# A gated GELU MLP on one core: eight transposing loads issued by ScalarE, 1 MB reloads ahead of the planes' stores, and four smaller moves in the order

## The chip, the cores and the metric

The kernel runs on one core of one Trainium2 chip. The metric is the device time of one execution in microseconds (us). Six actors matter: TensorE (PE, with its weight loads shown apart as PEld), VectorE (DVE), ScalarE (ACT), GpSimd (POOL), SyncE (SP, which issues nearly all DMAs in this kernel), and the 16 DMA engines that carry the transfers.

## The reference

For x of 2048 x 1024, W_gate and W_up of 1024 x 3584 and W_down of 3584 x 1024, all bf16:

```
g = x @ w_gate
u = x @ w_up
h = gelu_tanh(g) * u
out = h @ w_down
```

## The kernel before

The 2048 rows are handled in two passes of 1024 rows, and each pass in two halves c = 0, 1 of 512 rows. A pass has two stages: the units, which compute h for 256 columns of W_gate and W_up at a time (14 units), and `down`, which multiplies h by W_down. Within a stage the kernel doesn't do the plain eight block products of a 2 x 2 split of the matrices. It uses a scheme of seven products (Strassen's, in Winograd's form), and in some units and in one part of `down` a second level of it inside. So PE does fewer products, and the others form sums: VectorE and GpSimd make the operands (`s1`, `s2`, `s3`, `s4` of the weights, `t1` to `t4` of x; `s`, `q`, `m` in `down`), and ScalarE makes copies of PSUM banks (`snap`: u, p, u2, p5, z) and casts (`sa`, `tb`). Names of tiles in the profile are these names. Every matmul is of 128 x 128 by 128 x 512 and is recorded at line 145; VectorE's sums are recorded at line 121, GpSimd's at 124, ScalarE's copies at 133 or 138, its gelu at 213.

Most operands live in a ring of 36 slots of 2 KB a partition (`slot`, pool k) and one of 13 (pool s). A slot is given to the next tile when the last reader of the tile before it is done; where that reader is a store to DRAM, the next writer waits for the store.

*Order.* The work is emitted under a manual schedule: what an engine does stands in its queue in the order in which the program emits it, and an engine waits at each instruction for the semaphores that it needs. For `down` an agenda maps a step number to actions: `at(last, step, what, ...)` puts an action at a step of pass one (last = 0) or pass two (last = 1), and `step()` runs them in turn between the groups of products. The lists at the top give the steps: `LAST12` (`load12`, reloads of m, the sums of W_down that pass one left in DRAM as td), `LAST12S` (`make12`), `RAW73` (`fetch73`: the second halves of W_down), `LAST73` (`make73`: per j three VectorE sums s3, t3, s4 and one ScalarE cast tb). A transfer's completion is counted by one of eight semaphores, given out in turn over all DMAs that SP and ScalarE issue; a DMA waits for the one that had its semaphore before.

*The units that the change touches.* Pass two begins with unit 0's and unit 1's "raw" products (`raw_of`: plain first products of a unit whose sums aren't there yet; a closure finishes them with a sum, a gelu and a multiply). `prepare` runs inside a unit behind the p5 copies, `aside(part)` at marked points of it. `fetch_p5` reloads tiles that pass one stored in DRAM as pd. `need12(n)` fetches the n-th piece of W_down's first half (tile raw, line 689 in the page).

*The end of `down` in pass two.* It has the seven-product scheme over 14 values of j, and one of its seven products is itself done by the second level (`apart`). In order on PE: the raw first products; three groups of the q12 products; `apart` with its inner products K1, K2, K22, K3, K4 (with `step()` between); the remaining q12 products; then the q73 products for j = 0 to 13, and the last products bank by bank, each followed by a store of the output.

The four parts of the second-level product have to be transposed before they can be added to the output. `out(k, ...)` forms part k by two VectorE sums, `planes` splits the 32-bit numbers into two planes of 16 bits (a ScalarE copy) and stores them to DRAM (`pt[k]`, line 734); `turn_back(quad, n)` loads them back with a DMA that transposes (line 744; eight per quad, quad 0 holding parts 0 and 1, quad 1 parts 2 and 3); `join` puts the planes together again on ScalarE (tile gt). Parts 1 and 3 go to two fixed tiles (`pls`, `gs`), part 2, whose call gives no place, to tiles of the ring; part 0 is from pass one. `fetch_u3` reloads u3, the value to which gt is added (`put_0`, VectorE, tile st, and a store); `join_1` joins quad 1.

```
        out(1, Y, u, 0)
        inner(X, TI[K3], S1i, False, step=step)
        z = [snap(X[d], "z") for d in D]
        out(3, X, v, 2)
        inner(Y, TI[K4], S2i, True, step=step)
        out(2, Y, z)
```

`BIG12L = (5, 9)`: j = 5, 6 and j = 9, 10 are reloaded by one 1 MB load each (tile w of a pool of three, line 631 in the page), j = 7 and 8 by 512 KB loads (tile m, line 636), the others by 256 KB loads (tile q, line 642). The stores of the planes (`pt<-xT`, `pt<-pl`) and all these loads are in SP's one queue.

Of the kernel before, what the change touches and what calls it, by code (L numbers as in the profile page):

```python
# [10 lines left out]
def kernel(  # L11
# [23 lines left out]
    nc = tc.nc  # L35
# [36 lines left out]
    D2 = 2 * P  # L72
    ORD4 = [*range(0, NJ, 2), *range(1, NJ, 2)]
    MSTEPS = 17
    LAST12 = [14, 15, 16, 29, 30, 43, 43, 43, 44, 47, 47, 49, 50, 51]
    LAST12S = [16, 18, 20, 34, 37, 40, 43, 45, 47, 49, 51, 53, 55, 57]
    BIG12L = (5, 9)
    RAW73 = [41, 41, 41, 41, 48, 48, 50, 53, 55, 57, 60, 62, 64, 64]
    LAST73 = [52, 53, 55, 57, 59, 61, 63, 65, 66, 68, 70, 71, 72, 73]
    LATE3 = 6  # L80

# [28 lines left out]
    def slot(shape, dtype, name, sums=False):  # L110
        return (spool if sums else kpool).tile(shape, dtype, name=name, tag="s" if sums else "k")
# [8 lines left out]
    def dve(out, a, b, op):  # L120
        nc.vector.tensor_tensor(out=out, in0=a, in1=b, op=op)  # L121
# [14 lines left out]
    def snap(ps, name, at=None):  # L136
        t = slot([P, N], f32, name) if at is None else at
        nc.scalar.copy(out=t, in_=ps)  # L138
        return t
# [590 lines left out]
    def planes(k, d, at, pl=None):  # L730
        if pl is None:
            pl = slot([P, 2, N], u16, "pl")
        nc.scalar.copy(out=pl, in_=at.bitcast(u16).rearrange("p (n l) -> p l n", l=2))
        nc.sync.dma_start(
            out=pt[k].rearrange("(l d p) n -> d p l n", l=2, d=2)[d], in_=pl
        )
# [3 lines left out]
    def turn_back(quad, n):  # L740
        if n == 0:
            turned["tp", quad] = wpool.tile([P, NS, 2, N], u16, name="w")
        half, i = n // NS, n % NS
        nc.sync.dma_start_transpose(  # L744
            out=turned["tp", quad][:, i, half], in_=pt[2 * quad + half][:, i * P : (i + 1) * P]
        )

# [57 lines left out]
    def at(last, step, what, *args):  # L805
        agenda.setdefault((last, int(step)), []).append((what, args))

    for last in (False, True):
        if last:
            at(1, -1, load_ti, K1)  # L810
            at(1, -1, load_ti, K2)
            at(1, -1, load_a0)
        for n in range(NJ):
            at(last, max(-1, 2 * n - 8 if n < 10 else n + 1), need12, n)
        for j in range(NJ):
            at(last, (LAST12 if last else AT12)[j], load12, j, last)
            at(last, (LAST12S if last else AT12S)[j], make12, j, last)
            at(last, RAW73[j] if last else AT73[j] - 3, fetch73, j)
            at(last, (LAST73 if last else AT73)[j], make73, j, last)
# [7 lines left out]
    for i in range(NI):  # L827
        at(1, 2 * i, make_si, i)
    for n in range(2 * NS):
        at(1, 52 + n, turn_back, 0, n)  # L830
        at(1, 60 + n, turn_back, 1, n)
    for i in range(NS):
        at(1, 64 + 2 * i, fetch_u3, i)
        at(1, 68 + 2 * i, put_0, i)
        at(1, 70 + i, join_1, i)
    moves = [(c, ko) for ko in range(KH) for c in range(2)]
    moves += [(c, ko) for c in (1, 0) for ko in range(KH, NKB)]
    sa = {}
# [11 lines left out]
    def inner(ps, lhs, rhs, start, stop=True, step=None):  # L850
        for i in range(NI):
            if step and i % 2 == 0:
                step()
            for d in range(2):
                matmul(
                    ps[d], lhs[i][:, d * P : (d + 1) * P], rhs[i],
                    start and i == 0, stop and i == NI - 1,
                )

    def apart(c, step):  # L860
        X, Y = c[:2], c[2:]
        D = range(2)
        into(X, m1s)
        inner(Y, TI[K1], S1i, True, step=step)
        v = [snap(Y[d], "v") for d in D]
        inner(X, TI[K2], S2i, False, step=step)
        for i in range(NI):
            dve(S1i[i], A0[2 * i], h(1, 2 * i, 1), SUB)
        u = [snap(X[d], "u") for d in D]
        inner(Y, TI[K22], S4i, False, step=step)  # L870
        for i in range(NI):
            nc.scalar.copy(out=S2i[i], in_=h(1, 2 * i + 1, 1))

        pls = xpool.tile([P, 4, 2, N], u16, name="xT0")
        gs = xpool.tile([P, 4, N], f32, name="xT1")

        def out(k, ps, other, at=None):
            g = [slot([P, N], f32, "g") if at is None else gs[:, at + d] for d in D]
            for d in D:
                dve(g[d], ps[d], other[d], ADD)  # L880
            for d in D:
                planes(k, d, g[d], None if at is None else pls[:, at + d])

        out(1, Y, u, 0)
        inner(X, TI[K3], S1i, False, step=step)
        z = [snap(X[d], "z") for d in D]
        out(3, X, v, 2)
        inner(Y, TI[K4], S2i, True, step=step)
        out(2, Y, z)

    def down(ip, e, c, last, more):
        I = range(NS)
# [199 lines left out]
    def raw_of(u, e):  # L1092
        p1 = raw_products(e, K, xT, W(u))
        return lambda: finish_raw(u, K, p1)
# [33 lines left out]
    for ip in range(NPASS):  # L1128
        with tc.manual_schedule(engines={ENG.Activation}):
            if ip == 0:  # L1130
                ws = {1: w, 2: ahead}
                late = lambda: add(cc, nxt["p1"])
            else:
                fetch_ti(0), fetch_ti(1)
                raw_of(0, F)()
                rest(0)
                t["t3"] += t["how"]["t3"](t, range(2, KH))
                t.make("t4")
                raw_of(1, C)()
            for u in range(1 if ip == 0 else 0, NU):  # L1140
                if upgraded(u):
                    if u % 2:
# [52 lines left out]
                first = (ip, u) == (0, 1)  # L1195

                def prepare():
                    if first or (ip, u) == (1, 0):
                        pool_behind(t["t4"][-1])
                    if ip == 0 and u in (2, 3):  # L1200
                        lo_part(u - 2, 3, K)
                    if u + 1 < NU:
                        nxt["s"] = make_s(W(u + 1), pool, nxt.get("s"))
                    if (ip, u) == (0, FIRST - 2):
                        fetch_wd(JS[FIRST][:1])
# [10 lines left out]
                def aside(part):  # L1216
                    if first and part < 0:
                        rest_of_0(part + 2)
                    if ip == 1:
                        for i in {(0, 0): (2,), (1, 0): (3,), (1, 1): (4,), (2, 0): (5, 6)}.get((u, part), ()):  # L1220
                            fetch_ti(i)
                    if ip == 1 and part == 1:
                        if u == 0:
                            rest(1)
                        if u == 3:
                            send_a0()
                    if part == 0 and u + 2 < NU:
                        W(u + 2)
                        if ip and upgraded(u + 2):
                            fetch_p5(u + 2)  # L1230
                        if (ip, u) == (0, 1):
                            load_lo()
                    if first and part == 0:
                        t.make("t4")
# [84 lines left out]
```

## Time and profile before

| | |
|---|---|
| time, median of 3 runs | 545.5 us (544.61 to 547.37) |
| the profiled execution's own time | 548.82 us |
| its span in the profile | 547.0 us |
| mean granted clock of TensorE | 0.994 |
| PE busy | 531.8 us, 97% of the span, 2354 instructions |
| DVE, ACT, POOL busy | 404.8, 301.7, 268.4 us (74, 55, 49%) |
| DMA | 126.09 MB, mean 230 GB/s |
| largest kinds of load | W_down pieces x72 of 256 KB; W_gate and W_up x27 each of 512 KB |

The span is that of the profiled execution, and its rows are times from the span's start. Pass two's `down` takes the last part of it, and the end stage of which the prediction speaks, from the reloads of `apart` on, is about the last 75 us. PE's busy time counts a matmul's records until their modelled end, so a slow clock shows as busy time and not as idle. A row of the timeline gives start, length, engine, line, operation, out<-in, the count, and in brackets the idle time before it with what ended it. SPq is SP's queue, where a DMA's row is the issue; a row with DMA in place of the engine is the transfer itself.

### The profile page before, as it was taken

How to read it: one execution, taken by the hardware profiler on the slowest of the kernel's cores; microseconds unless marked ns; L12 is line 12 of the kernel's file. 1: busy time of each engine (PE TensorE's matmuls, PEld its weight loads, DVE VectorE, ACT ScalarE, POOL GpSimd, SP SyncE). 2: the span in 40 equal slices, each digit the busy share in tenths (PEclk: the TensorE clock that was granted, in tenths of full speed). 3: DMA queues.
4: the chain of work that ended last, by engine and by line, in shares of the span. 5: the costliest groups of instructions: out<-in, count | busy, mean ns of one | idle time of the engine just before them, and what ended most of it. 6: DMA issues, size and time to landing. Idle time of an engine off the chain costs nothing.

```text
span 547.0 us, 7735 instructions
## 1 busy us (share of the span) xinstructions
PE 531.8 (97%) x2354; PEld 375.4 (69%) x2375; DVE 404.8 (74%) x645; ACT 301.7 (55%) x544; POOL 268.4 (49%) x259
## 2 busy tenths in 40 slices
PE   8999999999999999999999999999999999997977
PEld 4568686868686864688867685776766854875855
DVE  2988768787777796659698786658657697895766
ACT  2567686968686821016666675565665611561560
POOL 1079968979698940000007978877897300000000
PEclk9999999999999999999999999999999999999988
DMA  9795227676666899999996899828443996589663
GB/s 242 160 245 162 77 80 267 204 278 208 215 237 235 285 386 382 326 303 216 246 303 212 277 333 347 232 58 232 118 114 115 315 353 227 192 286 318 166 145 125
DMA packets 141161, 126.09 MB, mean 230 GB/s; under 512 B 31680, under 2 KB 119232, under 8 KB 141120
## 3 DMA queue, kind: packets, MB, share of 16 engines
q1 hardware_dynamic: 141120, 125.60, 75.9%
q8 instruction: 19, 0.31, 0.2%
q14 instruction: 22, 0.18, 0.1%
HBM read 86.38 MB, written 31.06 MB: 215 GB/s over the span
## 4 chain that ended last, share of the span: by engine, by line
PE 86%; DMA 8%; DVE 2%; SPq 2%; issue 1%; ACT 0%; DVEq 0%; ACTq 0%
PE bank L145 86%; DMA raw<-in_w_down_dram 2%; DMA w<-td 2%; DVE q L121 1%; DMA hL<-w 1%; DMA pt<-pl 1%; DMA w<-in_w_up_dram 1%; DMA u<-ud 1%; SPq L618 0%; SPq L744 0%; DVE st L121 0%; SPq L992 0%; SPq L689 0%; ACT xT L138 0%; SPq L756 0%
## 5 line engine op out<-in xcount | busy, mean ns | idle before, releaser
L124 POOL TENSOR_TENSOR s<-w 128x512 fp32r<-128x512 bf16 x102 | 117.5, 1170 | 49.8 <-DMA w<-in_w_gate_dram 36.1
L145 PE MATMUL bank<-t,s 128*128 128x512 f32 x528 | 126.5, 392 | 1.1 <-ACT u L138 1.1
L145 PEld LDWEIGHTS bank<-t,s 128*128 128x128 f32 x528 | 99.0, 188 | 22.8 <-ACT u L138 1.5
L145 PE MATMUL bank<-xT,w 128*128 128x512 bf16 (+1 forms) x489 | 108.2, 376 | 1.4 <-DVE hT L121 0.3
L145 PEld LDWEIGHTS <-w 128*128 128x128 bf16 x504 | 47.8, 98 | 59.0 <-issue 5.4
L213 ACT ACTIVATE g<-sum 128x512 f32<-128x512 f32 x81 | 51.5, 636 | 65.3 <-DVE sum L121 63.0
L138 ACT COPY p<-bank 128x512 f32<-128x512 f32 x98 | 55.0, 590 | 46.6 <-PE bank L145 46.6
L145 PE MATMUL bank<-q 128*128 128x512 f32 x224 | 59.5, 404 | 5.3 <-DVE q L121 5.2
L121 DVE TENSOR_TENSOR hT<-g,bank 128x512 bf16<-128x512 f32 x72 | 49.0, 687 | 16.8 <-ACT g L213 11.1
L124 POOL TENSOR_TENSOR s<-w,s 128x512 fp32r<-128x512 bf16 x50 | 57.8, 1173 | 0.4
L124 POOL TENSOR_TENSOR s<-s,w 128x512 fp32r<-128x512 f32 x50 | 57.5, 1168 | 0.4
L121 DVE TENSOR_TENSOR bank<-bank,p 128x512 f32<-128x512 f32 x74 | 51.3, 695 | 6.5 <-PE bank L145 6.0
L145 PE MATMUL bank<-t,sa 128*128 128x512 f32 x216 | 54.9, 397 | 0.0
L145 PEld LDWEIGHTS bank<-q 128*128 128x128 f32 x224 | 42.6, 192 | 17.5 <-DVE q L121 8.1
L145 PE MATMUL bank<-tb,s 128*128 128x512 f32 x216 | 54.2, 393 | 0.0
L199 POOL COPY seen<-t 128x1 f32<-128x1 f32 x2 | 0.4, 183 | 108.4 <-DVE t L121 108.4
L145 PEld LDWEIGHTS bank<-t,sa 128*128 128x128 f32 x216 | 40.6, 188 | 9.1
L121 DVE TENSOR_TENSOR sum<-bank,p 128x512 f32<-128x512 f32 x54 | 37.0, 686 | 13.1 <-PE bank L145 11.4
L145 PEld LDWEIGHTS bank<-tb,s 128*128 128x128 f32 x216 | 40.6, 188 | 8.8
L138 ACT COPY u<-bank 128x512 f32<-128x512 f32 x62 | 35.3, 595 | 15.1 <-PE bank L145 11.7
L121 DVE TENSOR_TENSOR sum<-bank,u 128x512 f32<-128x512 f32 x27 | 18.5, 685 | 19.0 <-PE bank L145 16.3
L145 PE MATMUL bank<-raw,hT 128*128 128x512 bf16 x140 | 31.4, 379 | 1.1 <-DMA raw<-in_w_down_dram 0.9
(121 smaller groups left out, 727.6 us busy)
## 6 DMA issues: line engine op xcount, KB each, us to landing
raw<-in_w_down_dram SPq DMA_DIRECT2D x72, 256.0 KB, 5.9
w<-in_w_gate_dram SPq DMA_DIRECT2D x27, 512.0 KB, 4.5
w<-in_w_up_dram SPq DMA_DIRECT2D x27, 512.0 KB, 6.0
td<-m SPq DMA_DIRECT2D x11, 768.0 KB, 5.2
q<-td SPq DMA_DIRECT2D x28, 256.0 KB, 5.6
pd<-xT SPq DMA_DIRECT2D x10, 512.0 KB, 5.8
w<-td SPq DMA_DIRECT2D x5, 1024.0 KB, 9.4
p<-pd SPq DMA_DIRECT2D x20, 256.0 KB, 4.9
```

Of the source, the lines that this page charges most:

```text
L121: nc.vector.tensor_tensor(out=out, in0=a, in1=b, op=op)
L124: nc.gpsimd.tensor_tensor(out=out, in0=a, in1=b, op=op)
L138: nc.scalar.copy(out=t, in_=ps)
L145: nc.tensor.matmul(ps, lhsT=lhs, rhs=rhs, start=start, stop=stop, skip_group_check=True)
L199: nc.gpsimd.tensor_copy(out=seen, in_=tile[:, :1].bitcast(f32))
L213: nc.scalar.activation(g, src, ACT.Gelu_apprx_tanh)
```

## The change

Six edits to the order of emission, none to what PE does or to its order:

1. *Pass one's and pass two's first-half loads* (`need12`): the load n = 8 comes two steps earlier.
2. *Pass two, unit 0*: the finishing of unit 1's second raw product (its sums, its gelu, its multiplies) moves from the place right behind the products into unit 0's `prepare`, behind unit 0's p5 copies.
3. *Pass two, units 2 and 3*: `fetch_p5` for units 4 and 5 moves from `aside(0)` to `aside(1)`.
4. *Reloads in `apart`*: the two 1 MB loads are emitted right behind the inner products K22 and K3, and the 512 KB loads of j = 7 and 8 at step 41, ahead of the first store of the planes; before, they stood at steps 43 and 47.
5. *Part 2* goes to the places of part 1 in the two fixed tiles `gs` and `pls` in place of four tiles of the ring.
6. *The way back*: quad 0's eight transposing loads are issued by ScalarE, two a step in steps 52 to 55; quad 1's by SP a step earlier than before; `fetch73` comes up to four steps earlier; the four u3 loads come one a step in 66 to 69, and `put_0` and `join_1` alternate in steps 70 to 77.

```diff
--- before.py
+++ after.py
@@ -72,10 +72,10 @@
     D2 = 2 * P
     ORD4 = [*range(0, NJ, 2), *range(1, NJ, 2)]
     MSTEPS = 17
-    LAST12 = [14, 15, 16, 29, 30, 43, 43, 43, 44, 47, 47, 49, 50, 51]
+    LAST12 = [14, 15, 16, 29, 30, None, None, 41, 41, None, None, 49, 50, 51]
     LAST12S = [16, 18, 20, 34, 37, 40, 43, 45, 47, 49, 51, 53, 55, 57]
     BIG12L = (5, 9)
-    RAW73 = [41, 41, 41, 41, 48, 48, 50, 53, 55, 57, 60, 62, 64, 64]
+    RAW73 = [40, 40, 40, 40, 48, 48, 49, 50, 52, 53, 55, 57, 60, 60]
     LAST73 = [52, 53, 55, 57, 59, 61, 63, 65, 66, 68, 70, 71, 72, 73]
     LATE3 = 6
 
@@ -741,7 +741,8 @@
         if n == 0:
             turned["tp", quad] = wpool.tile([P, NS, 2, N], u16, name="w")
         half, i = n // NS, n % NS
-        nc.sync.dma_start_transpose(
+        queue = nc.sync if quad else nc.scalar
+        queue.dma_start_transpose(
             out=turned["tp", quad][:, i, half], in_=pt[2 * quad + half][:, i * P : (i + 1) * P]
         )
 
@@ -811,9 +812,10 @@
             at(1, -1, load_ti, K2)
             at(1, -1, load_a0)
         for n in range(NJ):
-            at(last, max(-1, 2 * n - 8 if n < 10 else n + 1), need12, n)
+            at(last, max(-1, (2 * n - 8 if n < 10 else n + 1) - 2 * (n == 8)), need12, n)
         for j in range(NJ):
-            at(last, (LAST12 if last else AT12)[j], load12, j, last)
+            if (LAST12 if last else AT12)[j] is not None:
+                at(last, (LAST12 if last else AT12)[j], load12, j, last)
             at(last, (LAST12S if last else AT12S)[j], make12, j, last)
             at(last, RAW73[j] if last else AT73[j] - 3, fetch73, j)
             at(last, (LAST73 if last else AT73)[j], make73, j, last)
@@ -827,12 +829,12 @@
     for i in range(NI):
         at(1, 2 * i, make_si, i)
     for n in range(2 * NS):
-        at(1, 52 + n, turn_back, 0, n)
-        at(1, 60 + n, turn_back, 1, n)
+        at(1, 52 + n // 2, turn_back, 0, n)
+        at(1, 59 + n, turn_back, 1, n)
     for i in range(NS):
-        at(1, 64 + 2 * i, fetch_u3, i)
-        at(1, 68 + 2 * i, put_0, i)
-        at(1, 70 + i, join_1, i)
+        at(1, 66 + i, fetch_u3, i)
+        at(1, (70, 72, 74, 76)[i], put_0, i)
+        at(1, (71, 73, 75, 77)[i], join_1, i)
     moves = [(c, ko) for ko in range(KH) for c in range(2)]
     moves += [(c, ko) for c in (1, 0) for ko in range(KH, NKB)]
     sa = {}
@@ -868,25 +870,26 @@
             dve(S1i[i], A0[2 * i], h(1, 2 * i, 1), SUB)
         u = [snap(X[d], "u") for d in D]
         inner(Y, TI[K22], S4i, False, step=step)
+        load12(BIG12L[0], True)
         for i in range(NI):
             nc.scalar.copy(out=S2i[i], in_=h(1, 2 * i + 1, 1))
 
         pls = xpool.tile([P, 4, 2, N], u16, name="xT0")
         gs = xpool.tile([P, 4, N], f32, name="xT1")
 
-        def out(k, ps, other, at=None):
-            g = [slot([P, N], f32, "g") if at is None else gs[:, at + d] for d in D]
+        def out(k, ps, other, at):
             for d in D:
-                dve(g[d], ps[d], other[d], ADD)
+                dve(gs[:, at + d], ps[d], other[d], ADD)
             for d in D:
-                planes(k, d, g[d], None if at is None else pls[:, at + d])
+                planes(k, d, gs[:, at + d], pls[:, at + d])
 
         out(1, Y, u, 0)
         inner(X, TI[K3], S1i, False, step=step)
+        load12(BIG12L[1], True)
         z = [snap(X[d], "z") for d in D]
         out(3, X, v, 2)
         inner(Y, TI[K4], S2i, True, step=step)
-        out(2, Y, z)
+        out(2, Y, z, 0)
 
     def down(ip, e, c, last, more):
         I = range(NS)
@@ -1136,7 +1139,7 @@
                 rest(0)
                 t["t3"] += t["how"]["t3"](t, range(2, KH))
                 t.make("t4")
-                raw_of(1, C)()
+                nxt["c11"] = raw_of(1, C)
             for u in range(1 if ip == 0 else 0, NU):
                 if upgraded(u):
                     if u % 2:
@@ -1195,6 +1198,8 @@
                 first = (ip, u) == (0, 1)
 
                 def prepare():
+                    if (ip, u) == (1, 0):
+                        nxt.pop("c11")()
                     if first or (ip, u) == (1, 0):
                         pool_behind(t["t4"][-1])
                     if ip == 0 and u in (2, 3):
@@ -1220,14 +1225,14 @@
                         for i in {(0, 0): (2,), (1, 0): (3,), (1, 1): (4,), (2, 0): (5, 6)}.get((u, part), ()):
                             fetch_ti(i)
                     if ip == 1 and part == 1:
+                        if u < 4 and upgraded(u + 2):
+                            fetch_p5(u + 2)
                         if u == 0:
                             rest(1)
                         if u == 3:
                             send_a0()
                     if part == 0 and u + 2 < NU:
                         W(u + 2)
-                        if ip and upgraded(u + 2):
-                            fetch_p5(u + 2)
                         if (ip, u) == (0, 1):
                             load_lo()
                     if first and part == 0:
```

## The prediction

> **What bounds the kernel now.** I read the page's busy shares and the summary of the chain that ended last, then the waits, then the timeline wherever TensorE (PE) waited.
>
> ```profile
> PE 531.8 (97%) x2354; PEld 375.4 (69%) x2375; DVE 404.8 (74%) x645; ACT 301.7 (55%) x544; POOL 268.4 (49%) x259
> ...
> PE 86%; DMA 8%; DVE 2%; SPq 2%; issue 1%; ACT 0%; DVEq 0%; ACTq 0%
> ```
>
> ```profile
> PE bank L145 <- DVE q L121: 5.2, 6, 1.9
> PE bank L145 <- DMA w<-td: 1.1, 1, 1.1
> PE bank L145 <- ACT u L138: 1.1, 1, 1.1
> PE bank L145 <- DMA raw<-in_w_down_dram: 0.9, 1, 0.9
> PE bank L145 <- DVE hT L121: 0.3, 1, 0.3
> ```
>
> PE is busy for 97% of the span, and its queue of products is the same in both programs (the change reorders only ScalarE, VectorE and SyncE). So what can be won is PE's waits for the others (us in total, times, longest): 0.9 + 1.1 + 0.3 = 2.3 us ahead of the end stage, and 1.1 + 5.2 = 6.3 in it. One loss has no wait; the table by stretches (busy time, then granted clock, DMA share, GB/s) shows it:
>
> ```profile
> 510.00:520.00 10.00, 10.00 (x46) 8.15 (x45) 5.94 (x10) 4.78 (x8) 0.00 (x0) 1.00 0.74 176
> 530.00:537.00 7.00, 6.06 (x14) 4.14 (x14) 7.00 (x13) 1.73 (x2) 0.00 (x0) 0.52 0.29 95
> ```
>
> The waits of that last stretch alone:
>
> ```profile
> PE bank L145 <- DVE q L121: 0.9, 2, 0.6
> ```
>
> From 530 to 537 the granted clock is 0.52. 14 products ran; at the rate of 510 to 520 (46 in 10 us) they take 3.0 us. Of the other 4.0, 0.9 are waits, which leaves some 3.0 to the slow clock. The ceiling of the change is 2.3 + 6.3 + 3.0 = 11.6 us.
>
> **Part by part. One load earlier in pass one.** PE's 0.9 is its wait for the fifth second-half load of W_down, which SyncE (SP) issued behind three stores. The change puts that load (n = 8) ahead of them.
>
> ```profile
> 204.75 1.42 SPq L618 DMA_DIRECT2D td<-m  x3
> 206.22 4.08 SPq L689 DMA_DIRECT2D raw<-in_w_down_dram  x4
> ```
>
> It is issued 1.47 us earlier (206.22 - 204.75), the stores 0.5 us later; VectorE, which waits for the stores' slots, feeds products several steps on. The next load keeps its place and is then the latest. 0 to 0.9, taken: 0.9.
>
> **Second raw product.** PE's 1.1 is a wait for ScalarE's copy u, and that stands behind a gelu:
>
> ```profile
> 291.50 0.63 ACT L213 ACTIVATE g<-sum 128x512 f32<-128x512 f32 x1 [4.69 <-DVE sum L121]
> 292.04 1.05 ACT L138 COPY u<-bank 128x512 f32<-128x512 f32 x2
> ```
>
> In the changed order both u copies and both p copies come before that gelu. The u copies need only products that ended before PE stopped. VectorE's multiply waits for the gelu about 0.6 us longer, and PE's next use of VectorE's sum is two groups of eight products (16 at 10 / 46 us, 3.5 us) on. GpSimd's first sum still waits for VectorE's t4, as before. Gain 1.1. **Loads of p5**: moved behind the stores of tid in units 2 and 3. PE's 0.3 (for VectorE's hT) came from a slot that such a store held, and the stores now go first; the p5 tiles are first read in unit 4. -0.3 to 0.3, taken: 0.3. Sum so far 2.3.
>
> **Reloads ahead of the planes' stores.**
>
> ```profile
> 469.49 1.92 SPq L662 DMA_DIRECT2D raw<-in_w_down_dram  x4
> 479.58 1.33 SPq L734 DMA_DIRECT2D pt<-xT  x2
> 481.00 0.43 SPq L631 DMA_DIRECT2D w<-td  x1
> ```
>
> ```profile
> 476.00:480.00 4.00, 4.00 (x20) 3.30 (x19) 2.88 (x5) 4.00 (x8) 0.00 (x0) 1.00 0.03 11
> 480.00:500.00 20.00, 18.76 (x81) 14.84 (x80) 14.06 (x23) 8.79 (x13) 0.00 (x0) 1.00 1.00 342
> ```
>
> ```profile
> 462.44 21.81 PE bank L145 x96
> 484.25 10.85 DMA w<-td
> ```
>
> Before, SP stood from 471.4 (469.49 + 1.92) at the first plane store, which waits for ScalarE until 479.58; both 1 MB loads and two 512 KB loads were queued behind it. The DMA engines idled from 476 to 480 (share 0.03), then ran full for 20 us (1.00, 342 GB/s), and the second 1 MB load, issued at 484.25, landed at 495.1: PE's wait of 1.1. In the changed order the 512 KB loads wait only for VectorE's sums, the first 1 MB load for the last product of K22, the second for that of K3. VectorE's rows date these:
>
> ```profile
> 473.30 0.68 DVE L121 TENSOR_TENSOR s<-a,hL 128x512 fp32r<-128x512 bf16 x1
> 473.90 0.68 DVE L121 TENSOR_TENSOR q<-hT,hL 128x512 fp32r<-128x512 bf16 x1
> 474.62 0.69 DVE L121 TENSOR_TENSOR q<-q,hT 128x512 fp32r<-128x512 f32 x1
> 477.09 1.29 DVE L121 TENSOR_TENSOR xT<-bank,u 128x512 f32<-128x512 f32 x2 [1.78 <-ACT s L872]
> ...
> 481.02 1.29 DVE L121 TENSOR_TENSOR xT<-bank,v 128x512 f32<-128x512 f32 x2
> ```
>
> The last sum s is done by 474; out(1) begins behind K22 at 477.1 and out(3) behind K3 at 481.0. So the second 1 MB load goes at 481 at the latest, 3 us earlier, and about 4 us x 342 GB/s = 1.4 MB of the queue ahead of it has landed by 480. It lands near 490, against a use that moves to 493.9 (495.1 less 1.1): the 1.1 goes. Price if not: 1.1.
>
> **Planes of the third part in pls and gs.** These tiles came from the ring of slots; VectorE's next operand then had to wait until the store left its slot:
>
> ```profile
> 500.55 0.69 DVE L121 TENSOR_TENSOR q<-hT,hL 128x512 fp32r<-128x512 bf16 x1 [6.32 <-DMA pt<-pl]
> ```
>
> With the parts in two fixed tiles that wait is gone; VectorE runs 6.3 us ahead, and two of PE's six waits for its q go:
>
> ```profile
> 502.03 1.21 PE L145 MATMUL bank<-q 128*128 128x512 f32 x4 [1.13 <-DVE q L121]
> ...
> 505.16 1.21 PE L145 MATMUL bank<-q 128*128 128x512 f32 x4 [1.00 <-DVE q L121]
> ```
>
> 1.13 + 1.00 = 2.1.
>
> **Eight transposes on ScalarE, u3 at the end.** PE's other four waits for q (5.2 - 2.1 = 3.1 us), and with them the slow clock (3.0), come from VectorE standing for its first u3:
>
> ```profile
> 524.03 0.69 DVE L121 TENSOR_TENSOR st<-gt,u 128x512 bf16<-128x512 f32 x1 [8.09 <-DMA u<-ud]
> ```
>
> ```profile
> L744 SPq DMA_TRANSPOSE w<-pt x16: 1127/1158/1258, 497.9 to 524.1; - x16
> ...
> DMA to landing us min/median/max: 2.7/3.1/5.2
> ```
>
> SP needs 1.158 us for each transposing load, 18.5 us for sixteen. Eight go to ScalarE, which has 9.3 us less idle then. But the order of the changed program gives SP's first transpose a wait for the landing of ScalarE's last ones, and behind it in SP's queue stand the last four W_down loads, seven more transposes, the four u3 loads and the stores of the output. So u3 is the thing that is late next:
>
> ```profile
> 487.56 2.18 ACT L677 CAST xT<-raw 128x512 fp32r<-128x512 bf16 x4
> ```
>
> ```profile
> 516.39 1.95 SPq L662 DMA_DIRECT2D raw<-in_w_down_dram  x4
> ```
>
> ```profile
> u<-ud SPq DMA_DIRECT2D x4, 256.0 KB, 3.7
> ```
>
> ```profile
> 543.62 0.69 DVE L121 TENSOR_TENSOR st<-bank,u 128x512 bf16<-128x512 f32 x1 [1.14 <-PE bank L145]
> ```
>
> From ScalarE's first transpose: eight issues 9.3, three casts among them 1.6 (2.18 / 4 each), landing 3.1, SP's four loads 1.95, its eight transposes 9.3, u3's landing 3.7: 29 us. It can begin at 489.7, when ScalarE is free (487.56 + 2.18), and at the latest at 497.9, where the first transpose was before; each waits for one of eight completion lanes, that is for loads issued just before, which land 4 us earlier than they did. I take 491, near the early end: u3 at 520. After it VectorE has ten operations at 0.6 us (473.90 - 473.30) before PE can start the last of the q73 products (j = 13): 526. PE ended at 543.6, where VectorE's last store begins. With 11.6 us gone it would end at 532.0 and want that one 36 products earlier, at 0.227 us (21.81 / 96) 8.2 us: 523.8. So 2.3 us of new wait; 1.0 from 489.7, 9.2 from 497.9. The price of an issue on ScalarE no row shows. Nearest is SP's 1.158; below it nothing is won past the 2.3; twice that costs 9.3 more.
>
> Sum: 2.3 + 1.1 + 2.1 + 3.1 + 3.0 = 11.6, less 2.3 is 9.3 us. The profiled execution took 548.82 (span 547.0 and 1.8 around it), so 539.5. The median of the runs, 545.5, is 3.3 below it; some of the waits may be the profiled execution's own, so I take 9.0 off the median: **536.5 us**.
>
> **Weighed against the Trainium skill.** The trace's clock fell after waits of at most 1.9 us at a time. The Trainium skill (TensorE: Matmul & The Clock Gate, Part 1) says that an idle window of about 3.4 us closes the gate; here the measurement differs, since no single wait is that long. By that rule a new wait of 2 to 6 us spread over several products costs no clock, and the first rival below would come out at 539.7. The added wait of SP's first transpose is what the skill (DMA: Bandwidth & Descriptors, on two transposing streams in flight) demands; no run here yet shows two streams.
>
> **Rivals.** *u3 too late* (0.18): lanes land late and ScalarE starts at 494.5. u3 at 523.5, VectorE at 529.5, 5.8 us of wait, and the clock falls again: 11.6 - 5.8 - 3.0 = 2.8 us, 542.7. For it: the chain of 29 us is all in order. Against: the idle DMA engines at 476 to 480. Its spread is 539 to 545, half of it past 0.5%.
>
> *ScalarE pays* (0.12, slower): an issue holds ScalarE 2.3 us. T from 491: 18.4 + 1.6 + 3.1 + 1.95 + 9.3 + 3.7 puts u3 at 529, VectorE at 535: 11.4 of wait and 3.0 of clock, 14.4 against 11.6, so 548.3. It turns at 2.0 us an issue. For it: nothing is shown of ScalarE's issues. Against: SP's sixteen lie within 1.127 and 1.258.
>
> *The end does not move* (0.10): the queue of loads is as full as before, or the end stage's waits are mostly the profiled execution's; only the 2.3 us ahead of it stay: 543.2, within 0.5%.
>
> **How the numbers follow.** Forecast 0.60, with its own range 533.5 (no new wait, 11.6 and a little off) to 539.5. The whole range goes to 543.5, over the third rival and most of the first; left out are the second and the upper tail of the first, under 0.2. A measurement of this kernel tells about 0.5% (2.7 us) from nothing. Faster 0.60 + 0.09 = 0.69, same 0.09 + 0.10 = 0.19, slower 0.12.
>
> **What would show it.** Right: no wait of PE for raw in pass one or for ScalarE's u; SP's m and w loads issued from 472 to 481; no wait of VectorE for pt; DMA_TRANSPOSE on ScalarE's queue at about 1.2 us each from 490 to 502; clock 1.00 to the end; PE's last product near 534. Wrong: a wait of VectorE for u3 over 5 us, transposes on ScalarE near 2 us or their first one past 496, PE waiting for ScalarE's copies of u2 or p5 behind them, or a clock of 0.5 again.

## The result, and the profile after

| | before | changed |
|---|---|---|
| median of 14 runs of each | 546.58 us (544.61 to 548.1) | 542.01 us (539.99 to 544.74) |
| ratio | | 0.9921, 95% interval 0.9903 to 0.9939 |
| profiled execution, its own time | 548.82 | 539.99 |
| its span, its mean clock | 547.0, 0.994 | 538.2, 1.000 |
| second profiled execution: time, span, clock | 547.38, 545.6, 0.994 | 542.64, 540.9, 0.994 |

The change gains 4.6 us (0.8%). That is the way that was forecast and inside the stated range, but only about half of the 9.0 us. The two profiled executions of the first pair are 8.8 us apart, nearly the forecast's 9.3, but that is luck: before's was slower than each of its 14 other runs, the changed kernel's the fastest of its 14. The second pair is 4.7 apart, like the medians.

The page of the changed kernel, busy shares and the summary of the chain:

```profile
PE 529.5 (98%) x2375; PEld 374.2 (70%) x2375; DVE 404.0 (75%) x645; ACT 302.2 (56%) x544; POOL 268.3 (50%) x259
...
PE 91%; DVE 3%; SPq 3%; DMA 1%; issue 1%; ACT 1%; DVEq 0%; ACTq 0%
```

TensorE's waits in the changed kernel from 480 us on are one line. In this execution the three waits ahead of the end stage, the one for the 1 MB reload and the two behind VectorE's wait for pt are gone:

```profile
PE bank L145 <- DVE q L121: 3.9, 3, 2.1
```

The table by stretches; the first two rows answer to those of before:

```profile
476.00:480.00 4.00, 4.00 (x19) 3.31 (x18) 3.93 (x7) 3.73 (x6) 0.00 (x0) 1.00 0.96 364
480.00:500.00 20.00, 19.81 (x86) 15.69 (x85) 18.89 (x32) 6.01 (x9) 0.00 (x0) 1.00 1.09 298
510.00:520.00 10.00, 9.94 (x43) 7.73 (x42) 0.00 (x0) 2.25 (x4) 0.00 (x0) 1.00 0.59 122
527.00:534.00 7.00, 7.00 (x32) 5.73 (x31) 7.00 (x13) 0.81 (x1) 0.00 (x0) 1.00 0.55 186
```

The DMA engines, idle from 476 to 480 before (0.03), now run (0.96). From 510 to 520 VectorE does nothing (0.00): it stands at its first u3, which this row of the timeline shows,

```profile
520.06 0.69 DVE L121 TENSOR_TENSOR st<-gt,u 128x512 bf16<-128x512 f32 x1 [10.56 <-DMA u<-ud]
```

and SyncE's rows show why:

```profile
503.49 1.16 SPq L745 DMA_TRANSPOSE w<-pt  x1
504.75 1.94 SPq L662 DMA_DIRECT2D raw<-in_w_down_dram  x4
506.74 9.75 SPq L745 DMA_TRANSPOSE w<-pt  x7
516.59 1.95 SPq L757 DMA_DIRECT2D u<-ud  x4
```

SyncE's eight transposes and four loads go first, and u3 leaves at 516.59. VectorE's last store, which marks TensorE's end, begins 14.7 us after the u3 addition:

```profile
534.78 0.69 DVE L121 TENSOR_TENSOR st<-bank,u 128x512 bf16<-128x512 f32 x1 [0.23 <-PE bank L145]
```

So u3 is late next, as the forecast and its first rival said, and the time, 542.0, is near that rival's (542.7), though not by its dates: u3 came at 520, not at 523.5. (The third rival's 543.2 is near it too, but by that one nothing in the end stage would have changed.) The experiments ask what the gain came from, and what the wait for u3 costs.

### The profile page after: what moved, and what is told of

Its sections match the earlier page's. It is cut to its first block, busy times and chain, and to the rows that moved or that the text cites. A ratio compares the mean times of both kernels' runs of the same rounds, so it can differ in the third digit from the quotient of the medians.

```text
span 538.2 us, 7762 instructions
## 1 busy us (share of the span) xinstructions
PE 529.5 (98%) x2375; PEld 374.2 (70%) x2375; DVE 404.0 (75%) x645; ACT 302.2 (56%) x544; POOL 268.3 (50%) x259
## 4 chain that ended last, share of the span: by engine, by line
PE 91%; DVE 3%; SPq 3%; DMA 1%; issue 1%; ACT 1%; DVEq 0%; ACTq 0%
PE bank L145 91%; DVE q L121 2%; SPq L745 2%; DMA w<-in_w_up_dram 1%; DVE xT L121 1%; DMA u<-ud 1%; ACT s L875 0%; SPq L995 0%; SPq L757 0%; DVE st L121 0%; ACT u L138 0%; SPq L662 0%; SPq L1014 0%; DVEq L121 0%; ACTq L138 0%
## 5 line engine op out<-in xcount | busy, mean ns | idle before, releaser
L145 PE MATMUL bank<-xT,w 128*128 128x512 bf16 (+1 forms) x504 | 110.4, 376 | 0.1
L145 PE MATMUL bank<-q 128*128 128x512 f32 x224 | 57.4, 394 | 4.1 <-DVE q L121 3.9
L133 ACT CAST tb<-raw 128x512 fp32r<-128x512 bf16 x20 | 12.4, 627 | 36.5 <-DMA raw<-in_w_down_dram 30.1
L133 ACT CAST sa<-w 128x512 fp32r<-128x512 bf16 x54 | 30.7, 616 | 2.7 <-DMA out_dram<-st 2.7
```

The costliest lines, as they stand in the source:

```text
L133: nc.scalar.copy(out=t, in_=src)
L145: nc.tensor.matmul(ps, lhsT=lhs, rhs=rhs, start=start, stop=stop, skip_group_check=True)
```

## The experiments

Each ratio is to runs of before that stood beside the experiment on the same chip; their medians lay between 545.35 and 546.81. Two kernels measured on different chips are best compared by their ratios. An interval in brackets behind a ratio is its 95% interval.

### Second executions of both

No edit.

> The kernel before once more, unchanged, for a second profiled execution beside the one that the forecast was summed from. Theory A (the waits of the first profile are there in every execution): TensorE waits again about 0.9 for raw, 1.1 for u, 0.3 for hT, 1.1 for the 1 MB reload and 5.2 for q, 8.6 us in all. Theory B (some of them are that execution's own): the 0.9 and the 0.3 are smaller or gone, as they are in the run with the three edits ahead of the end stage undone, the other 7.4 within 1.5 us. The clock lies between 0.994 and 1.00.

> The changed kernel once more, unchanged, for a second profiled execution. Theory A: VectorE stands 9 to 12 us for its first u3 and TensorE waits 3.5 to 5 us for q, again between 517 and 527; where its mean clock is under 1.00, the stretch of low clock lies right behind those waits. Theory B (the first profile's waits aren't typical): under 2 us of waits for q.

The two took 547.38 and 542.64 us. TensorE's waits in the second execution of before:

```profile
PE bank L145 <- DVE q L121: 5.6, 5, 2.5
PE bank L145 <- ACT u L138: 1.1, 1, 1.1
PE bank L1054 <- PEq L1303: 0.8, 1, 0.8
PE bank L145 <- DMA w<-td: 0.6, 1, 0.6
PE bank L145 <- DMA raw<-in_w_down_dram: 0.4, 1, 0.4
```

and of the changed kernel:

```profile
PE bank L145 <- DVE q L121: 2.5, 3, 1.6
PE bank L145 <- DMA q<-td: 0.9, 2, 0.5
PE bank L1057 <- PEq L1308: 0.8, 1, 0.8
PE bank L145 <- DMA raw<-in_w_down_dram: 0.4, 1, 0.4
```

A wait of 0.4 for raw is there although the first edit is in place, so that this edit isn't shown to remove such waits. For line 145 that is 7.7 (5.6 + 1.1 + 0.6 + 0.4) against 3.8 (2.5 + 0.9 + 0.4): 3.9 of the 4.7 us. In the first pair it was 8.6 against 3.9, 4.7 us; the rest of its 8.8 is mostly clock, (1.000 - 0.994) x 547 = 3.3. The second execution of the changed kernel has the slow stretch again; it begins among the three waits behind the late u3, which end at 522.72, 524.53 and 526.93:

```profile
510.00:520.00 10.00, 10.00 (x45) 8.11 (x44) 0.79 (x2) 3.38 (x4) 0.00 (x0) 1.00 0.58 105
524.00:531.00 7.00, 6.14 (x14) 4.36 (x15) 7.00 (x13) 4.51 (x5) 0.00 (x0) 0.52 0.25 86
```

14 products in 7 us at 0.52, as in the first profile of before. Over its 14 runs the changed kernel's clock is 0.9957 in the mean, an estimated loss of 2.3 us (0.0043 x 541); that of before beside the experiments is 0.995 to 0.997, 1.7 to 3 us. So on average the change doesn't win the clock back. The estimate is rough: of the 72 runs of before beside the experiments, the 35 with a clock of 0.993 or 0.994 took 547.2 us in the mean and the 15 with 1.000 took 545.0, which is 2.1 us and not 3.3.

### The wait for u3 taken away

Edits on the changed kernel, `put_late`, `u3_first` and both together:

```diff
 # put_late
-        at(1, (70, 72, 74, 76)[i], put_0, i)
-        at(1, (71, 73, 75, 77)[i], join_1, i)
+        at(1, 73 + i, put_0, i)
+        at(1, 74 + i, join_1, i)
 # u3_first
-        at(1, 66 + i, fetch_u3, i)
+        at(1, 57 + i // 2, fetch_u3, i)
```

> The changed kernel with VectorE's four u3 additions moved behind the operands of j = 11, 12 and 13 (ScalarE's joins follow them); nothing else differs. Theory A (u3 is late next): in the changed kernel's trace VectorE stands 10.6 us for the first u3 and TensorE waits 3.9 us for the operands behind it, and the slow clock of most of its executions follows from that wait. Then no wait of TensorE for q is left, the clock is 1.00, and the median falls by 4 to 6 us, to 536 to 538. Theory B (what is missing to the forecast is only that the profiled execution of before was a slow one): the waits have other causes too, the median stays within 1.5 us of 542.0.

> The changed kernel with the four loads of u3 issued by SyncE ahead of its eight transposes, not behind them; nothing else differs but the slots that this moves. Theory A: u3 lands before VectorE wants it (509), the wait of 10.6 us falls to what the joins of the first quad leave, under 2 us; 3 to 6 us faster than the changed kernel, 536 to 539. Theory B: within 1.5 us of 542.0. Theory C (the ring of slots): four slots taken some 10 us earlier hold up VectorE's operands of j = 5 to 8, 541 to 545.

> The changed kernel with both: u3 loaded ahead of the second quad, and VectorE's u3 additions behind the operands of j = 11 to 13. Theory A (TensorE has no wait left with either): the two don't add up, 535 to 536.5, and TensorE's end is the end. Rival (the stores of the output and the joins are next): the later additions push VectorE's last stores past TensorE's end, 536.5 to 538.

They took 536.84 us (ratio 0.9829, 0.9803 to 0.9856), 535.78 (0.981, 0.9784 to 0.9835) and 535.26 (0.9804, 0.9775 to 0.9832). Theory A held each time; the second is 0.2 us below its range. With u3 first, all that is left of TensorE's waits in the whole profiled execution is

```profile
PE bank L1057 <- PEq L1308: 0.8, 1, 0.8
```

and the clock is 0.999 or more in every run, 0.998 or more with the additions late. The two moves don't add up, as they shouldn't if each removes the same wait and leaves TensorE with its own work. So the late u3 costs the changed kernel 5 to 6 us; TensorE's waits behind it are 3.9 and 2.5 in the two profiles, the clock's loss 2.3 in the mean.

### Who issues the transposes, and the whole sixth edit

```diff
 # sp_issues_all, on the changed kernel (u3_first_sp_all: with u3 first as well)
-        queue = nc.sync if quad else nc.scalar
+        queue = nc.sync
 # way_back_undone: this, and RAW73 and the steps of turn_back, fetch_u3, put_0 and join_1 as before
```

> The changed kernel with the eight transposing loads issued by SyncE at the same steps as ScalarE does; nothing else differs. By the forecast's chain (eight issues on ScalarE, then their landing, then SyncE's eight): without a second issuer there is no wait for a landing between the two sets of eight (in the changed trace SyncE's first transpose starts at 503.5, 0.1 after ScalarE's last one landed, 4.7 after it was issued), so SyncE gets u3 out at 514 in place of 516.6, and the time is 1 to 3 us shorter than 542. Rival: the split is what gains, SyncE alone is 9.3 us longer at it, u3 is issued at 521 or later and the time is 3 to 5 us longer, 545 to 547.

> The changed kernel with the whole sixth edit undone: all sixteen transposes on SyncE at the old steps, the old steps for the second halves of W_down, for u3, for VectorE's u3 additions and for the second quad's joins. By the forecast's sum the sixth edit brings 3.1 of waits and 3.0 of clock less 2.3: 546. By the runs so far (SyncE issuing all took 541.2, u3 at the same place): it brings nothing that the others don't, 541.5 to 543.5.

> The changed kernel with u3 loaded ahead of the second quad, and all sixteen transposing loads issued by SyncE. Theory A (issuing from ScalarE moves nothing, since the second eight have to wait for the first eight's landing anyway: in the run with SyncE issuing all, u3 was issued at 517.0, and with the split at 516.6): within 1 us of the split's 535.8. Rival (the split gains once u3 is out of the way): the second quad lands later, ScalarE's joins and VectorE's last stores with it, 537.5 to 540.

They took 541.17 us (0.9912, 0.9888 to 0.9936), 540.04 (0.9893, 0.9867 to 0.992) and 537.36 (0.9841, 0.9811 to 0.9872). With SyncE issuing all sixteen, u3 leaves when it leaves in the changed kernel, and not at 514 as expected:

```profile
517.03 1.95 SPq L757 DMA_DIRECT2D u<-ud  x4
```

517.03 stands against 516.59. Two queues bring nothing here: ScalarE's first transpose starts 3.8 us earlier than SyncE's does alone (488.11 against 491.90), but from the end of ScalarE's last issue (496.14 + 2.58) to SyncE's first transpose (503.49) 4.8 us pass, in which nobody issues one; alone, SyncE is at its ninth at 504.37. The expected gain of 1 to 3 us from one queue isn't shown either; 0.8 lies within the intervals. The sixth edit as a whole brings nothing that can be shown: undone, the kernel is no slower (540.04, below both expectations), and the first u3 addition is 4 us earlier than in the changed kernel,

```profile
515.74 0.69 DVE L121 TENSOR_TENSOR st<-gt,u 128x512 bf16<-128x512 f32 x1 [9.28 <-DMA u<-ud]
```

though by ratio the time is only 1.5 us less (0.0028 x 546; the intervals overlap). TensorE's waits for q, 2.9 us in this run, stay: in the old order VectorE's next addition waits again, 1.0 us for ScalarE's tb. With u3 out of the way the split may be worth 1.6 us (537.36 against 535.78, between the two expectations); the intervals overlap.

### The reloads

```diff
 # only_reloads, on the kernel before (reloads_behind: the reverse, on the changed kernel)
-    LAST12 = [14, 15, 16, 29, 30, 43, 43, 43, 44, 47, 47, 49, 50, 51]
+    LAST12 = [14, 15, 16, 29, 30, None, None, 41, 41, None, None, 49, 50, 51]
...
         inner(Y, TI[K22], S4i, False, step=step)
+        load12(BIG12L[0], True)
...
         inner(X, TI[K3], S1i, False, step=step)
+        load12(BIG12L[1], True)
```

> The changed kernel with the four reloads (two of 1 MB, two of 512 KB) put back behind the stores of the planes; nothing else differs. By the forecast's sum: TensorE's wait for the 1 MB load is back, 0.6 to 1.1 us, and everything in SyncE's queue behind it, u3 too, is some 3 us later: 543 to 546. Rival (the end hangs on u3 alone, and the planes' stores, which now go first, let the transposes start as early): the wait is swallowed by the one for u3, within 0.7 us of 542.

> The kernel before with one edit: the two 1 MB and the two 512 KB reloads ahead of the planes' stores. Theory A (the reloads carry the gain since they bring the whole of SyncE's queue behind them forward, u3 too): SyncE's transposes start 3 to 4 us earlier, VectorE's first u3 with them; TensorE's 0.6 to 1.1 for the 1 MB load goes; 541 to 543. By the forecast's sum: the 1.1 alone, 544.5 to 545. Rival (VectorE's wait for part 2's stores, which stays, holds the rest back): 544 to 546.

> The changed kernel with u3 loaded ahead of the second quad, and the four reloads behind the planes' stores again. Theory A (what the reloads bring beside their own wait is that ScalarE's transposes start earlier, behind which its casts stand): in the run with the reloads behind, TensorE waited 0.8 for the 1 MB load and 3.0 for operands behind ScalarE's cast, both ahead of u3; 3.8 us, 539 to 540.5. By the forecast's sum: 1.1 alone, 536.5 to 537.

They took 545.88 us (0.999, 0.9969 to 1.0012), 542.57 (0.9916, 0.989 to 0.9943) and 541.12 (0.9902, 0.9876 to 0.9928). This one edit alone is as fast as the whole change (0.9916 against 0.9921), and without it the other five are worth nothing that can be measured (0.999). Which of the four loads it takes was not tried apart. In `only_reloads` the first plane store is issued at 478.44, about when it was (479.58), but the loads are ahead of it, the first at 470.47:

```profile
470.47 2.15 SPq L636 DMA_DIRECT2D m<-td  x2
476.10 0.37 SPq L631 DMA_DIRECT2D w<-td  x1
478.44 1.33 SPq L734 DMA_DIRECT2D pt<-xT  x2
479.86 0.49 SPq L631 DMA_DIRECT2D w<-td  x1
```

What follows is earlier too. VectorE's waits for pt and for its first u3 in this run:

```profile
494.96 0.69 DVE L121 TENSOR_TENSOR q<-hT,hL 128x512 fp32r<-128x512 bf16 x1 [1.86 <-DMA pt<-pl]
...
518.25 0.69 DVE L121 TENSOR_TENSOR st<-gt,u 128x512 bf16<-128x512 f32 x1 [7.89 <-DMA u<-ud]
```

The wait for pt is 1.86 where it was 6.32, though part 2 is still in the ring, and no wait of TensorE follows it; u3 comes at 518.25 (524.03 before). The chain of the kernel before shows how the 1 MB load holds that store:

```profile
484.25 10.85 DMA w<-td
495.10 0.02 issue
495.12 0.02 SPq L734
495.13 0.03 issue
495.16 5.37 DMA pt<-pl
500.53 0.02 issue
500.55 0.70 DVE q L121
```

The store of part 2's planes (line 734) reads nothing of the 1 MB load, but is the eighth transfer after it in SyncE's queue, so it has the same one of the eight semaphores and waits for that load: it starts at 495.16, when the load has landed, and VectorE's operand waits for the store. With the load issued at 479.86 the store starts at 489.48. In TensorE's waits the one edit shows as 3.9 us: the 1.1 for the load, the 2.1 behind pt, and 0.7 of the waits behind u3, which are 2.4 where they were 3.1. Against the second execution of before it is 3.8 (0.6, 2.2 and 1.0).

With the reloads behind, on the changed kernel, ScalarE's transposes are late instead, and its casts stand behind them:

```profile
494.71 0.62 ACT L677 CAST xT<-raw 128x512 fp32r<-128x512 bf16 x1 [9.71 <-DMA raw<-in_w_down_dram]
494.82 5.16 ACTq L745 DMA_TRANSPOSE w<-pt  x4
500.02 0.62 ACT L677 CAST xT<-raw 128x512 fp32r<-128x512 bf16 x1 [4.69 <-issue]
```

```profile
491.26 3.92 PE L145 MATMUL bank<-w,q 128*128 128x512 f32 x16 [0.84 <-DMA w<-td]
502.02 1.17 PE L145 MATMUL bank<-q 128*128 128x512 f32 x4 [3.02 <-DVE q L121]
```

The 0.84 is the wait for the load, as priced, and the 3.02 is put down to an operand behind VectorE's wait for the cast. With u3 first it is again 0.8 and 3.0, the second now put down to a 256 KB load (q):

```profile
PE bank L145 <- DMA q<-td: 3.0, 1, 3.0
PE bank L145 <- DMA w<-td: 0.8, 1, 0.8
```

In that run VectorE doesn't wait for the cast. The load is issued at 498.11, right behind the landing of one of ScalarE's transposes (issued at 492.00, landed at 498.05), and lands at 501.66. So a late start of ScalarE's transposes holds up SyncE's loads too, and not only ScalarE's casts, as theory A had it; for the 3.02 of the run without u3 first, which of the two decides isn't settled. By the ratio the reloads are worth 5.0 us here (0.0092 x 546), more than these 3.8 us of waits, and above what either theory said; the clock is 0.996 to 0.997 in its five runs.

### Part 2's tiles, and the three early edits

In the first two runs, `out` is as before too, and a call without a place takes slots of the ring.

```diff
 # part2_ring and u3_first_part2_ring: on the changed kernel, without and with u3 first
-        out(2, Y, z, 0)
+        out(2, Y, z)
 # head_undone and u3_first_head_undone: need12(8), raw_of(1, C) and fetch_p5 as before
```

> The changed kernel with the tiles of part 2 taken from the ring of slots again; nothing else differs. By the forecast's sum: VectorE's wait of 6 us for the stores (pt) is back, and TensorE's two waits for q behind it, 2.1 us: 544. Rival (the end hangs on u3, which SyncE and ScalarE bring at the same time as in the changed kernel): TensorE comes 2.1 us later to its wait for u3, which is 2.1 us shorter for that; within 0.7 us of 542.

> The changed kernel with u3 loaded ahead of the second quad, and part 2 in tiles of the ring again. If the forecast's term is right where u3 hides nothing: TensorE's two waits behind VectorE's wait for pt are back, 2.1 us, 537.5 to 538.5 against 535.8. Rival (the waits are hidden by something else than u3): under 1 us, 535.5 to 536.8.

> The changed kernel with the three edits ahead of the end stage undone (the load n = 8, the finishing of unit 1's second raw product, the loads of p5). If the 2.3 us of waits in the profiled execution of before are there in every execution, the time is 2.3 us longer than the changed kernel, 544.3, and the three waits are back in its trace. Rival: the waits are given back later or are that execution's own, under 1 us longer.

> The changed kernel with u3 loaded ahead of the second quad, and the three edits ahead of the end stage undone. By the forecast's sum 2.3 us, 538. By the second profiled execution of before (1.1 for u, 0.4 for raw, nothing for hT) and the run with them undone (0.9): 1.1 to 1.5 us, 537 to 537.3.

| undone | changed kernel | with u3 first |
|---|---|---|
| none | 542.01 (0.9921) | 535.78 (0.981) |
| part 2's tiles | 542.83 (0.9942, 0.9918 to 0.9966) | 537.49 (0.9834, 0.9811 to 0.9858) |
| the three early edits | 542.88 (0.9945, 0.9923 to 0.9967) | 538.01 (0.9853, 0.982 to 0.9887) |

With part 2 in the ring both waits of TensorE are back, 0.94 and 1.01 in the run with u3 first:

```profile
PE bank L145 <- DVE q L121: 2.0, 2, 1.0
```

The ratios say 0.0021 x 546 = 1.1 us on the changed kernel, 0.0024 x 546 = 1.3 with u3 first; each lies within the intervals. So neither the full 2.1 us nor a hiding behind u3 is shown. And the two waits are there only beside other edits of the change: in `only_reloads` and in the last run below, which have part 2 in the ring too, VectorE waits 1.86 and 1.42 us for pt and TensorE not at all behind it. With part 2 in the ring of the changed kernel VectorE comes to such a slot at 489.3 (488.7 with u3 first), not at 493.1 as in `only_reloads`, and waits 4.9 (4.7). Which edit brings it there earlier no run tells apart.

Of the three early waits only the one for u (1.1) is in both traces with them undone; raw and hT are in some executions and not in others. The costs by ratio, 1.3 and 2.3 us, are too uncertain to tell 1.1 from 2.3; the six runs behind the 538.01 lie between 536.27 and 541.38, two of them with a clock of 0.995 and 0.996.

### u3 alone, and two moves alone

```diff
 # only_u3_first, on the kernel before
-        at(1, 64 + 2 * i, fetch_u3, i)
+        at(1, 58 + i // 2, fetch_u3, i)
 # reloads_u3_first_put_late: this, the reloads as above, and
-        at(1, 68 + 2 * i, put_0, i)
-        at(1, 70 + i, join_1, i)
+        at(1, 73 + i, put_0, i)
+        at(1, 74 + i, join_1, i)
```

> The kernel before with one edit: the four loads of u3 are issued by SyncE ahead of the second quad's transposes (steps 58 and 59 in place of 64 to 70). Theory A (u3's place in SyncE's queue is what the end hangs on, before the change too): VectorE's wait of 8.1 us for u3 and TensorE's 3.1 us behind it go, and the clock's loss (0.003 of the span in the middle, 1.6 us) with them: 541 to 542, as fast as the whole change. Rival (the joins of the first quad are as late as u3: SyncE issues sixteen transposes from 497.9 on): VectorE waits for gt in its place, 544 to 546.

> The kernel before with two moves: the four reloads ahead of the planes' stores, and u3 loaded ahead of the second quad with VectorE's u3 additions (and the second quad's joins) behind the operands of j = 11 to 13. Theory A (reloads and u3 are all there is in the end stage): TensorE has no wait left in it, only the 1.1 for u and up to 0.9 for raw ahead of it; 536.5 to 538.5. Rival (with SyncE issuing all sixteen, the second quad's joins and VectorE's last stores come behind TensorE's end): 538.5 to 541.

They took 545.86 us (1.0, 0.9983 to 1.0017) and 537.79 (0.9845, 0.9809 to 0.9881). The first came out as its rival said: u3 is there in time, and VectorE waits as long for gt:

```profile
525.43 0.69 DVE L121 TENSOR_TENSOR st<-gt,u 128x512 bf16<-128x512 f32 x1 [7.83 <-ACT gt L749]
```

for on ScalarE the join of the second quad stands ahead of that gt, and waits for SyncE's transposes:

```profile
523.16 1.17 ACT L749 COPY w<-w 128x1024 uint16<-128x1024 uint16 x1 [6.18 <-DMA w<-pt]
```

u3 and the second quad come from one queue; to move the one is of use only if nobody stands for the other. The two moves together (with VectorE's u3 additions and the joins late), without the other edits, give twice the gain of the whole change and lie in theory A's range. TensorE's waits in that run are two from ahead of the end stage and one at the start:

```profile
PE bank L145 <- ACT u L138: 1.1, 1, 1.1
PE bank L1057 <- PEq L1306: 0.8, 1, 0.8
PE bank L145 <- DMA raw<-in_w_down_dram: 0.4, 1, 0.4
```

## Why the prediction was right in its chain and wrong in its sum

*The chain to u3* held: u3 at 520 forecast, VectorE's first addition at 520.06; TensorE's end at 534.3 (532.0 + 2.3) forecast, 534.78 measured. That it held to 0.1 us is partly luck, for within it terms were off and cancelled: ScalarE began 2.9 us earlier (488.1, not 491), but its last load landed 4.7 us behind the end of its issue (498.7 to 503.4), not 3.1, and SyncE's eight transposes and four loads took 13.0 us (503.49 to 516.49), not 11.3. An issue on ScalarE, which no row had shown, took 1.28 us; "ScalarE pays" fell with that. The wait of VectorE for u3, 10.56 us, is what the forecast itself named as a sign of being wrong (over 5 us), though its own chain came to it: VectorE, free at 515.94 before and 6.3 us ahead, would stand from 509.6 to 520.

```profile
L745 ACTq DMA_TRANSPOSE w<-pt x8: 1236/1282/1321, 488.1 to 497.4; - x8
L745 SPq DMA_TRANSPOSE w<-pt x8: 1136/1258/2062, 503.5 to 515.2; - x8
```

SyncE's queue was free from 499.7 on (four loads, issued from 495.32 in 4.36 us), and its first transpose stood until ScalarE's last had landed, 503.4, 3.7 us. This is the wait that the Trainium skill (DMA: Bandwidth & Descriptors, on two transposing streams in flight) demands; the trace agrees. It takes back what ScalarE's earlier start gains.

*What failed* is the sum, in two of its terms: the slow clock counted as won (3.0), and the new wait (2.3). The first pair of profiles has lost all 8.6 us of old waits, as forecast. But the new wait is 3.9 us and not 2.3 (2.5 in the second profile), and on average the clock wasn't won: 9.3 less 1.6 less 3.0 is 4.7, and 4.6 was measured. That this fits to 0.1 us is luck, since the second pair has 7.7 of waits less 3.8, 3.9 us.

The 3.0 us of clock came from one execution and were taken off the median of others. That execution's clock was 0.994; before's runs lose 1.7 to 3 us in the mean, by the estimate above. The changed kernel loses 2.3, with a clock below 1.000 in 12 of 14 runs, while in the three kernels that only take the late u3 out of the way it is 0.998 or more in every run. So the new wait goes with a slow clock as the old one did, which the forecast had kept for its first rival alone. The allowance of 0.3 for "the profiled execution's own" was too small as well, for that execution was 2.2 above the median. For the profiled execution itself the working gave 539.5, and the changed kernel's took 539.99; that match is luck, since it was one of only two runs with a full clock.

*The gain was put down to the wrong edits.* The reloads were given 1.1 us and gain as much alone (4.6) as the whole change, for they bring forward what stands behind them in SyncE's queue: the stores that hold VectorE's slot (6.32 to 1.86 us), and the transposes (the first at 492.31, not 497.90). Part 2's tiles (2.1) then have about 1.2 left to win beside the other edits, and the sixth edit (3.1 + 3.0 - 2.3 = 3.8) nothing. The forecast had the row for this, DMA engines idle at 0.03 from 476 to 480, and priced it for one load only; the chain that ties part 2's store to that load was in the same profile.

*The early edits* (2.3) cost 1.3 us by the ratios when undone and 2.3 with u3 first, within the intervals; only the 1.1 for u is shown in each trace.

## What to carry to other kernels

When a queue stands at a store that waits for another engine, price what moving the store is worth by all that is queued behind it, and not by the first load alone. A wait that goes is won only up to the next late item of the same queue: write down when that item comes, and ask whether it can be taken out of the way (here by moving four loads, 6 us) before spending edits on how fast the queue is issued. Take clock losses from several runs' mean clocks and not from one profile, and count them as won only if no wait of that kind is left.

## What was not expected of the hardware

In the second execution of the changed kernel the products slow down after two waits, 1.59 and 0.61 us (four products in 1.20 us, then in 2.07), and the clock stays near 0.52 for some 7 us. In the first it stayed at 1.00 after 2.07, 0.60 and 1.19 us:

```profile
522.72 1.20 PE L145 MATMUL bank<-q 128*128 128x512 f32 x4 [1.59 <-DVE q L121]
524.53 2.07 PE L145 MATMUL bank<-q 128*128 128x512 f32 x4 [0.61 <-DVE q L121]
```

The window of about 3.4 us that the Trainium skill (TensorE: Matmul & The Clock Gate, Part 1) gives for a closing gate isn't what the trace shows here: no single wait was that long, the slow stretch followed two shorter ones, and in another execution such waits left the clock at 1.00. What decides is open; no run varied the waits alone.

The sixteen transposing loads of the changed kernel take longer to land than those of before (2.7/3.1/5.2):

```profile
DMA to landing us min/median/max: 2.6/4.6/6.3
```

The eight issued by ScalarE are the slow ones, 5.9 us in the median against 2.7 for SyncE's eight. They run beside 256 KB loads (the 1 MB loads have landed by 486, before the first of them starts), and the DMA engines are busier then (share 1.09 from 480 to 500, 0.59 from 510 to 520). But the first eight take only 3.9 us when SyncE issues them, in `sp_issues_all`. Whether the queue or the traffic makes the difference isn't shown.
